# Fetching the first MLP's inputs apart from the addition of their halves, and starting those additions later in attention

## The chip, the cores and the metric

The kernel runs on one core of a Trainium2 chip. A core has engines that run side by side, each with its own queue of instructions in order: TensorE (PE: matmuls; its weight loads are listed as PEld), VectorE (DVE), ScalarE (ACT), GpSimd (POOL), and SyncE (SP), whose queue here only issues DMA transfers between DRAM and the core's memory. Engines wait for each other through semaphores. The metric is the device time of one execution in microseconds.

## The reference

Attention with a memory term over 4 batches, 8 heads, 576 positions and head width 64, then two MLPs over the 2304 tokens (512 wide, 2048 hidden), the first with an ELU and the second with a leaky ReLU. All inputs are float32.

```python
scores = scale * q @ k^T                      # causal mask
a = softmax(scores); local = a @ v
q_p = phi(q)                                  # elu(q) + 1
mem_out = (q_p @ M_prev) / (q_p . z_prev + 1e-06)
x = g * mem_out + (1 - g) * local             # 2304 x 512
h = x @ moe_w_in;  x = where(h > 0, h, exp(min(h, 0)) - 1) @ moe_w_out
h = x @ moe2_w_in; out = max(0.01 * h, h) @ moe2_w_out
```

## The kernel before

**Numbers.** Products are made from float32 operands cut into a high part (`xh`, `gh`, ...) and the rest (`xl`, `gl`, ...), with three matmuls for one product (high by high, by the weights' rest, rest by high). Batch 0's attention runs in plain float32 (`V32 = 1`), the other batches' attention with the cut.

**Attention.** Each batch is one token tile `ti` of 576 tokens; its 8 heads are taken as 4 pairs `hp`. Per head and group of queries there are scores (L426, L427), the exponentials on DVE (L429), transposes of the probabilities (L455), and the product with the values in `pv` (L522), whose accumulator `po` goes through a copy `xp` to DRAM. In batch 0 that is ACT's copy and a write into `xm` (L527). In the other batches the accumulator holds two products whose sum is the output; DVE copies it (L529) and SP writes it into `xq` (L530), one buffer per head of the pair, so the reader has to add two halves. `k_unit`, `q_unit` and `qp_unit` prepare keys and queries (L292 to L341; DVE makes the rests there, `kl` L300, `qs` L341, `qpl` L248).

**The first MLP's first part.** It takes 7 of the 16 hidden blocks (`NFA`) and is filled into attention, because PE is not kept busy by attention alone. `phase1_units(ti)` makes a list of units for one batch's two parts of 288 tokens. Before the change, each part has:

- `u_x`: fetch, addition and cut. Batch 0: one DMA `x<-xm` (L675, 576 KB). Others: four DMAs, two halves into `x` (L681) and two into `y` (L682), 288 KB each, then four additions `x<-x,y` on DVE (L684), one per 128 rows of the 512. Then `split_x`: four casts `xh` on ACT (L239 inside `copy`), four subtractions `xl` on POOL (L609), and the writes of both to DRAM for the MLP's second part (L670).
- seven `u_h`: 12 matmuls each into a bank `pm` (L616), then the ELU (ACT twice at L629, DVE at L630) and the cut of the result into `gh` and `gl`.
- four `u_o`: 21 matmuls each (L644), a copy and a write of `ys` (L697).

The tiles `x` and `y` have one buffer each (`mtile("x", 1, ...)`), so a part's fetch into them waits until the part before has been read out of them.

**What sets the order.** The attention units come as one list with a cost each; `pos` is the sum of the costs so far (in ns of PE). When a batch's last attention unit is passed (`done`), its MLP units are appended to `fill`, due at `pos + DELAY` (13000). From that point each attention unit adds `c * rate` to a credit, and a unit of `fill` is emitted as soon as it is due and its cost is covered; units with cost 0, as `u_x`, go at once when they are first in the list. Units of `fill` are emitted with a raised priority (`FILL_OFF = 20`). That is the order in which the code is written. The Tile scheduler then orders each engine's queue itself, by priority and by its own times of when operands are ready, so the order in the program can differ from the order of emission.

The lines that place the units:

```python
        if done is not None:
            fill += [(pos + DELAY, c2, u2) for c2, u2 in phase1_units(done)]
        if fill and fill[0][0] <= pos:
            credit += c * rate
        while fill and fill[0][0] <= pos and fill[0][1] <= credit:
            _, c2, u2 = fill.pop(0)
            credit -= c2
            with tc.high_priority(offset=FILL_OFF):
                u2()
```

What is left of `fill` when attention ends is run with the loading of more weights; then come the rest of the first MLP and the second MLP, to the end.

## Time and profile before

| | us |
|---|---|
| median of three runs | 1096.52 |
| lowest, highest | 1096.45, 1099.43 |
| the profiled execution | 1098.26 |
| its span (first to last instruction) | 1096.2 |
| PE busy in it | 1057.6 (96%) |
| DVE, ACT, POOL busy | 600.3, 484.8, 530.6 |
| mean granted clock of TensorE, share of full | 0.995 |

The profiled execution is one more run, with 2.06 us outside its span. The busy share is an average over stages. The first 385 us or so hold attention with the first MLP filled in between; after it there is little but MLP. So the table of windows (busy time by stretch), the timelines of PE, DVE and SP with what ended each wait, and the DMA issues with their time to landing are what to read for this change.

### The profile page before, as it was taken

What the parts mean: (1) busy time and instruction counts of PE and PEld (TensorE: products, weight loads), DVE (VectorE), ACT (ScalarE), POOL (GpSimd) and SP (SyncE); (2) the same over time, 40 slices, a digit from 0 to 9 for tenths busy, and PEclk for the clock granted to TensorE, in tenths of its full rate; (3) what the DMA queues carried; (4) which work ended last, traced back from release to release, by engine and by line L of the source; (5) the groups of instructions that cost most, each with busy time, mean ns of one, the idle gap of its engine ahead of it and who ended that gap; (6) DMA issues with size and microseconds to landing.
All of it is one profiled execution on the core that took longest, in us unless ns stands there. A gap on an engine that the chain in (4) does not pass through costs nothing.

```text
span 1096.2 us, 17406 instructions
## 1 busy us (share of the span) xinstructions
PE 1057.6 (96%) x5904; PEld 912.7 (83%) x5904; DVE 600.3 (55%) x1398; ACT 484.8 (44%) x1169; POOL 530.6 (48%) x674
## 2 busy tenths in 40 slices
PE   6998899989998999999999999999999999999997
PEld 3777789979998999978877889888888888888896
DVE  6889987778878857566574314664321222232232
ACT  5988877777877645444343223432211110111110
POOL 7675675667667626455453224755422322222221
PEclk9999999999999999999999999999999999999999
DMA  7753643564365139665653304331200100010010
GB/s 181 189 144 91 188 115 99 124 169 145 78 178 156 59 81 271 225 215 185 219 189 119 98 18 116 135 116 39 77 1 1 58 20 1 1 39 1 1 39 20
DMA packets 151576, 115.05 MB, mean 105 GB/s; under 512 B 81728, under 2 KB 144192, under 8 KB 151488
## 3 DMA queue, kind: packets, MB, share of 16 engines
q1 hardware_dynamic: 151488, 113.95, 35.5%
q8 instruction: 47, 0.77, 0.3%
q14 instruction: 41, 0.34, 0.1%
HBM read 78.52 MB, written 31.85 MB: 101 GB/s over the span
## 4 chain that ended last, share of the span: by engine, by line
PE 73%; DMA 8%; DVE 7%; POOL 3%; ACT 3%; SPq 3%; issue 3%; DVEq 0%; POOLq 0%; ACTq 0%
PE pm L616 17%; PE sc L876 14%; PE tp L616 13%; PE sc L644 8%; PE po L876 4%; PE pm L644 4%; PE po L522 3%; PE tp L455 3%; PE po L644 2%; DMA wraw<-in_moe_w_out_dram 2%; DMA x<-xq 2%; SPq L212 2%; PE sc L426 1%; PE sc L427 1%; PE pm L522 1%
## 5 line engine op out<-in xcount | busy, mean ns | idle before, releaser
L623 POOL TENSOR_TENSOR gl<-e,gh 128x512 fp32r<-128x512 f32 (+2 forms) x181 | 199.8, 1108 | 369.8 <-DVE gh L241 291.9
L616 PE MATMUL tp<-xw,w 128*128 128x512 f32 (+1 forms) x504 | 145.4, 371 | 0.9 <-DVE e L630 0.9
L616 PE MATMUL pm<-xw,w 128*128 128x512 f32 (+1 forms) x496 | 143.9, 371 | 0.0
L876 PE MATMUL sc<-w,gh 128*128 128x512 f32 x448 | 137.7, 393 | 0.0
L449 POOL TENSOR_SCALAR pt<-pt,rs,omg 128x128 f32<-128x128 f32 (+4 forms) x160 | 102.7, 651 | 28.0 <-DVE rs L444 25.7
L616 PEld LDWEIGHTS tp<-xw,w 128*128 128x128 f32 x504 | 91.3, 188 | 19.7 <-DVE e L630 1.7
L644 PE MATMUL sc<-gh,w 128*128 128x512 f32 (+2 forms) x438 | 106.0, 343 | 1.1 <-DVE st L857 0.7
L616 PEld LDWEIGHTS pm<-xw,w 128*128 128x128 f32 x496 | 90.5, 188 | 18.5
L434 ACT ACTIVATE pt<-pt,mx 128x128 f32<-128x128 f32 (+4 forms) x160 | 93.2, 585 | 22.7 <-DVE mx L429 22.1
L876 PEld LDWEIGHTS sc<-w,gh 128*128 128x128 f32 x448 | 83.1, 188 | 17.9
L616 PE MATMUL tp<-xv,w 128*128 128x512 f32 (+1 forms) x252 | 93.2, 370 | 0.0
L616 PE MATMUL pm<-xv,w 128*128 128x512 f32 (+1 forms) x248 | 92.0, 371 | 0.0
L616 PE MATMUL pm<-xh,w 128*128 128x288 f32 x368 | 80.2, 305 | 9.1 <-DVE e L630 5.7
L635 ACT ACTIVATE e<-pm 128x512 f32<-128x512 f32 (+1 forms) x40 | 22.2, 556 | 150.3 <-PE pm L616 149.1
L455 PE MATMUL tp<-ident,pt 128*128 128x128 f32 x480 | 80.1, 276 | 8.0 <-DVE al L248 3.1
L241 DVE CAST gh<-e 128x512 fp32r<-128x512 f32 (+2 forms) x146 | 77.9, 537 | 16.9 <-PE po L644 4.2
L137 POOL TENSOR_TENSOR w<-wm,w 128x512 fp32r<-128x512 f32 x50 | 66.1, 1344 | 43.4 <-ACT w L239 43.4
L876 PE MATMUL sc<-w,gl 128*128 128x512 f32 x224 | 85.4, 393 | 0.0
L644 PEld LDWEIGHTS sc<-gh,w 128*128 128x128 f32 x438 | 74.6, 188 | 12.2 <-issue 1.5
L636 DVE TENSOR_TENSOR e<-tp,e 128x512 f32<-128x512 f32 (+1 forms) x40 | 25.5, 637 | 107.2 <-ACT e L635 107.1
L636 DVE TENSOR_TENSOR e<-pm,e 128x512 f32<-128x512 f32 (+1 forms) x40 | 25.5, 637 | 105.8 <-ACT e L635 105.8
L429 DVE CUSTOM_DVE_ANT_0 pt<-sc,mask 128x128 f32<-128x128 f32 (+4 forms) x160 | 69.4, 446 | 8.6 <-PE sc L427 4.3
(155 smaller groups left out, 2407.9 us busy)
## 6 DMA issues: line engine op xcount, KB each, us to landing
wraw<-in_moe_w_in_dram SPq DMA_DIRECT2D x32, 512.0 KB, 4.1
wraw<-in_moe_w_out_dram SPq DMA_DIRECT2D x32, 512.0 KB, 5.3
xh<-xh SPq DMA_DIRECT2D x8, 576.0 KB, 3.3
xl<-xl SPq DMA_DIRECT2D x8, 576.0 KB, 3.9
ys<-st SPq DMA_DIRECT2D x32, 144.0 KB, 3.0
x1s<-st SPq DMA_DIRECT2D x36, 128.0 KB, 1.9
x<-x1s SPq DMA_DIRECT2D x9, 512.0 KB, 3.9
out_dram<-st SPq DMA_DIRECT2D x36, 128.0 KB, 1.7
```

The costliest lines, as they stand in the source:

```text
L137: nc.gpsimd.tensor_tensor(out=w[:, 1, a], in0=t[:, a], in1=_f(w)[:, 0, a], op=ALU.subtract)
L241: (nc.vector if eng == "V" else nc.gpsimd).tensor_copy(dst, src)
L429: nc.vector.tensor_tensor_reduce(out=pt[0:m, k0:k0 + n], in0=sc[0:m, 0:n], in1=mk, op0=ALU.add, op1=ALU.min, scale=-0.125, scalar=mx[0:m, ...
L434: nc.scalar.activation(out=pt[0:m, 0:nk], in_=pt[0:m, 0:nk], func=AF.Exp, scale=-1.0, bias=mx[0:m, last:last + 1], accum_out=self.pd["ss"] ...
L449: nc.gpsimd.tensor_scalar(out=pt, in0=pt, scalar1=rs[0:m, i:i + 1], scalar2=omg[0:m, h:h + 1], op0=ALU.mult, op1=ALU.mult,)
L455: nc.tensor.transpose(dst, self.p[c][:, k0:k0 + kn], ident)
L522: nc.tensor.matmul(po[:, a:b], w, x, start=i == 0, stop=i == len(mms) - 1)
L616: nc.tensor.matmul(ph, wi[:, wj, kc, :], xx[:, kc, :], start=n_mm == 0, stop=n_mm == 11)
L623: nc.gpsimd.tensor_tensor(out=gl, in0=g, in1=_f(gh), op=ALU.subtract)
L636: nc.vector.tensor_tensor(out=t, in0=ph, in1=t, op=ALU.max)
L644: nc.tensor.matmul(py, wo[:, wj, ec * P:(ec + 1) * P], gg, start=opens and f == first and n_mm == 0, stop=closes and f == last and n_mm == 2,)
L876: nc.tensor.matmul(pos[tb], gg[:, tb * P:(tb + 1) * P], wo[:, wj, :], start=f == 0 and n_mm == 0, stop=f == NF - 1 and n_mm == 2,)
```

## The change

Fetching and adding become two functions. `u_load` allocates the tiles and issues the DMAs. `u_x` does the additions (for batches with halves), the cut and its writes. The list of units begins with `u_x` of the first part; the second part's `u_load` stands after the first part's second `u_h` (f = 1), and its `u_x` after the first part's sixth (f = 5). Before, the second part's `u_x` with all its DMAs stood behind the four `u_o` of the first. `phase1_units` now returns the first part's `u_load` beside the list, and the main loop calls it at the moment the batch's attention is done, at ordinary priority. From batch 1 on the list is due at `pos + LATE` (20000) instead of `pos + DELAY` (13000); batch 0 keeps 13000. The number of instructions of each kind is the same.

```diff
+    LATE = 20000.0
...
-            def u_x(pi=pi, o=o, w=w, st=st):
-                def split():
-                    st["x"] = split_x(xt, w, pi % 2)
...
-                xt = mtile("x", 1, F32, (NKC, NW))[:, :, 0:w]
-                if ti < V32:
-                    nc.sync.dma_start(xt, xm_scr[ti][:, :, o:o + w])
-                    split()
-                    return
...
-                for c in range(NKC):
-                    nc.vector.tensor_tensor(out=xt[:, c], in0=xt[:, c], in1=x2[:, c], op=ALU.add)
-                split()
+        mine = [(pi, o, w, {}) for pi, (pt, o, w, _) in enumerate(parts) if pt == ti]
+
+        def u_load(pi, o, w, st):
+            xt = st["t"] = mtile("x", 1, F32, (NKC, NW))[:, :, 0:w]
+            if ti < V32:
+                nc.sync.dma_start(xt, xm_scr[ti][:, :, o:o + w])
+                return
+            x2 = st["t2"] = mtile("y", 1, F32, (NKC, NW))[:, :, 0:w]
+            for j in range(2):
+                ps, pz = slice(64 * j, 64 * j + 64), slice(64 - 64 * j, 128 - 64 * j)
+                nc.sync.dma_start(xt[ps], xq_scr[ti][j][ps, :, o:o + w])
+                nc.sync.dma_start(x2[ps], xq_scr[ti][j][pz, :, o:o + w])
+
+        def u_x(pi, o, w, st):
+            xt = st["t"]
+            if ti >= V32:
+                for c in range(NKC):
+                    nc.vector.tensor_tensor(out=xt[:, c], in0=xt[:, c], in1=st["t2"][:, c], op=ALU.add)
+            st["x"] = split_x(xt, w, pi % 2)
+            for n in range(2):
+                nc.sync.dma_start(xp_scr[n][pi], _f(st["x"][n]))
+            st["g"] = {}
+
+        units = [(0, lambda: u_x(*mine[0]))]
+        for k, (pi, o, w, st) in enumerate(mine):
...
             for f in range(NFA):
                 units.append((HC * 12 * w / 2.4, lambda f=f, u=u_h: u(f)))
+                if k + 1 < len(mine) and f == 1:
+                    units.append((0, lambda k=k: u_load(*mine[k + 1])))
+                if k + 1 < len(mine) and f == NFA - 2:
+                    units.append((0, lambda k=k: u_x(*mine[k + 1])))
...
-        return units
+        return lambda: u_load(*mine[0]), units
...
-            fill += [(pos + DELAY, c2, u2) for c2, u2 in phase1_units(done)]
+            fetch, more = phase1_units(done)
+            fetch()
+            start = pos + (DELAY if done < V32 else LATE)
+            fill += [(start, c2, u2) for c2, u2 in more]
```

What this makes of the program's order is shown at three places. A row is a line of the kernel, an operation, what it writes and reads, and its shape. Lines of the changed kernel are one higher up to L660 (L528 is L527 of before, L617 is L616, L645 is L644, L249 is L248, L430 is L429), the fetches are L666, L671 and L672, the additions L678, the writes of the cut L681.

**Batch 0's first fetch, SP's queue.** `xm` is what batch 0's attention writes, `x` the tile of the MLP's input; `kn`, `vn`, `qn` and `kk` belong to the attention of batch 1, and `xq` is its output. Before:

```order
L212 DMA vn<-in_v_dram 128x2x64 x3
L530 DMA xq_0_86<-xp 128x320
L217 DMA vn<-in_v_dram 64x2x64 x2
L227 DMA zb<-in_z_prev_dram 128x256
L530 DMA xq_1_87<-xp 128x256
L675 DMA x<-xm_80 128x4x288
L212 DMA kn<-in_k_dram 128x3x64 x2
L530 DMA xq_1_87<-xp 128x320
```

After:

```order
L213 DMA kn<-in_k_dram 128x3x64
L528 DMA xm_80<-xp 64x320
L300 DMA kk_1537<-kk_1537 64x256
L300 DMA kk_1537<-kk_1537 64x320
L666 DMA x<-xm_80 128x4x288
L213 DMA kn<-in_k_dram 128x3x64
L300 DMA kk_1538<-kk_1538 64x256
L531 DMA xq_0_86<-xp 128x256
```

The fetch `x<-xm` stood 17 rows behind the last write of `xm`, between `xq` writes of batch 1's second head; now it stands three rows behind it.

**The end of batch 0's MLP and the beginning of batch 1's, PE and DVE.** On PE, L644 (after: L645) are the last output matmuls of batch 0, and L616 with `xh0_3624` (after: L617 with `xh0_3774`) the first of batch 1's; the others are attention's. PE before:

```order
L644 MATMUL pm_3589<-gh_3061,w4_792 128x288 x2
L644 MATMUL pm_3589<-gl_3062,w4_792 128x288
L644 MATMUL pm_3589<-gh_3130,w5_904 128x288 x2
L644 MATMUL pm_3589<-gl_3131,w5_904 128x288
L644 MATMUL pm_3589<-gh_3192,w6_1009 128x288 x2
L644 MATMUL pm_3589<-gl_3193,w6_1009 128x288
L616 MATMUL pm_3666<-xh0_3624,w0_200 128x288 x2
L522 MATMUL po_3423<-qph_3037,ms0_164 128x320
L522 MATMUL po_3423<-qpl_3038,ms0_164 128x320
```

PE after, where batch 0's matmuls end:

```order
L645 MATMUL pm_3595<-gl_3137,w5_904 128x288
L329 MATMUL po_3045<-ident_66,ph_e_2823 128x128 x2
L645 MATMUL pm_3595<-gh_3198,w6_1009 128x288 x2
L645 MATMUL pm_3595<-gl_3199,w6_1009 128x288
L427 MATMUL sc_3388<-kk0_3160,qs0_3228 128x448
L428 MATMUL sc_3388<-kl0_1_175,qs0_3228 128x448
L456 MATMUL tp_3299<-ident_66,pt21_182 128x128
L456 MATMUL tp_3299<-ident_66,pt3_3153 128x128
L456 MATMUL tp_3299<-ident_66,pt4_3202 128x128
```

PE after, 26 rows further down, where batch 1's begin:

```order
L456 MATMUL tp_3373<-ident_66,pt3_3153 128x128
L456 MATMUL tp_3373<-ident_66,pt4_3202 128x128
L523 MATMUL po_3109<-qph_3043,ms0_164 128x256
L523 MATMUL po_3109<-qpl_3044,ms0_164 128x256
L523 MATMUL po_3109<-dh2_152,vv_2844 128x256 x2
L523 MATMUL po_3109<-dl2_154,vv_2844 128x256 x2
L293 MATMUL sc_3574<-ident_66,kn_3269 128x128 x3
L617 MATMUL pm_3812<-xh0_3774,w0_200 128x288 x2
L617 MATMUL pm_3874<-xh0_3774,w1_390 128x288 x2
```

L616 stood directly behind the last L644; now 33 rows with 40 matmuls of attention lie between. On DVE, the additions of batch 1's first part (L684, after: L678) in the same place, with their neighbours. DVE before:

```order
L529 COPY xp_3219<-po_3207 128x320
L248 TENSOR_TENSOR al_3298<-tp_3333,ah_3297 128x320
L429 ISA pt4_3387,mx_3388<-sc_3389,mask_128 128x288
L429 ISA mx_3388 128x1
L248 TENSOR_TENSOR dl2_154<-tp_3361,dh2_152 128x384
L429 ISA pt0_3450,mx_3451<-sc_3452,mask_128 128x128
L429 ISA mx_3451 128x1
L429 ISA pt4_3387,mx_3388<-sc_3393,mask_128,mx_3388 128x288
L429 ISA mx_3388 128x1
L684 TENSOR_TENSOR x_3614<-x_3614,y_3615 128x288 x4
L529 COPY xp_3353<-po_3346 128x256
```

DVE after:

```order
L430 ISA pt0_3456,mx_3457<-sc_3458,mask_128 128x128
L430 ISA mx_3457 128x1
L430 ISA pt1_3478,mx_3479<-sc_3480,mask_128 128x256
L430 ISA mx_3479 128x1
L249 TENSOR_TENSOR al_3304<-tp_3339,ah_3303 128x320
L678 TENSOR_TENSOR x_3030<-x_3030,y_3031 128x288 x4
L249 TENSOR_TENSOR qpl_3044<-po_3092,qph_3043 128x320
L430 ISA pt21_182,mx_3550<-sc_3551,mask_128 64x320
L430 ISA mx_3550 64x1
```

Both copies `xp` in the piece of before belong to batch 2. The last one of batch 1, whose write the fetch has to wait for, stands 47 rows ahead of the additions before and 24 rows ahead of them after, outside of both pieces. Behind the additions stood a copy `xp`; now `qpl` stands there, which PE's L523 of the piece above reads.

**Batch 1's second part, DVE.** L684 (after: L678) are its additions, L630 (after: L631) the ELU of the first part's hidden blocks. DVE before:

```order
L429 ISA pt3_3821,mx_3822<-sc_3823,mask_128 128x448
L429 ISA mx_3822 128x1
L684 TENSOR_TENSOR x_4507<-x_4507,y_4508 128x288 x2
L630 SCALAR_TENSOR_TENSOR e_3852<-e_3852,pm_3839 128x288
L429 ISA pt4_3828,mx_3829<-sc_3830,mask_128 128x288
L429 ISA mx_3829 128x1
L684 TENSOR_TENSOR x_4507<-x_4507,y_4508 128x288 x2
L248 TENSOR_TENSOR al_3743<-tp_3738,ah_3742 128x320
```

DVE after:

```order
L249 TENSOR_TENSOR al_3706<-tp_3701,ah_3705 128x320
L430 ISA pt4_3786,mx_3787<-sc_3792,mask_128,mx_3787 128x288
L430 ISA mx_3787 128x1
L445 RECIPROCAL rs_3739<-rs_3739 128x2
L678 TENSOR_TENSOR x_3895<-x_3895,y_3896 128x288 x4
L631 SCALAR_TENSOR_TENSOR e_3954<-e_3954,pm_3941 128x288
L430 ISA pt0_3845,mx_3846<-sc_3847,mask_128 128x128
L430 ISA mx_3846 128x1
```

The additions stood two and two around an ELU; now they are in one piece, between attention's L445 and an ELU. Counted on PE's queue, 9 matmuls stood between the last DMA into `x` and the first of these additions, and now 47.

## Rows read from the trace of the kernel before

**Rows 1.** Page, busy time of the engines, share of the span, instructions.

```profile
PE 1057.6 (96%) x5904; PEld 912.7 (83%) x5904; DVE 600.3 (55%) x1398; ACT 484.8 (44%) x1169; POOL 530.6 (48%) x674
```

**Rows 2.** Windows: busy (count) of PE, PEld, DVE, ACT, POOL; clock, DMA share, GB/s.

```profile
102.00:120.00 18.00, 14.99 (x98) 12.27 (x98) 17.56 (x59) 13.08 (x38) 11.75 (x23) 1.00 0.56 140
160.00:200.00 40.00, 39.88 (x310) 39.48 (x310) 30.44 (x97) 29.71 (x86) 25.28 (x42) 1.00 0.38 100
216.00:234.00 18.00, 15.18 (x112) 13.90 (x111) 11.49 (x37) 11.30 (x34) 9.47 (x17) 1.00 0.72 191
234.00:250.00 16.00, 13.40 (x88) 12.51 (x87) 13.16 (x39) 13.26 (x38) 11.65 (x17) 0.89 0.62 158
318.00:330.00 12.00, 10.88 (x84) 10.45 (x83) 9.06 (x27) 7.14 (x22) 9.17 (x13) 1.00 0.78 216
330.00:342.00 12.00, 9.17 (x60) 8.92 (x60) 8.97 (x22) 7.90 (x23) 7.51 (x12) 0.86 0.85 242
```

**Rows 3.** SP timeline, last writes and fetches of batches 0 and 1: start, duration, transfer.

```profile
101.74 0.48 SPq L527 DMA_DIRECT2D xm<-xp  x1
...
116.09 0.55 SPq L675 DMA_DIRECT2D x<-xm  x1
...
199.72 0.32 SPq L530 DMA_DIRECT2D xq<-xp  x1
...
214.12 0.54 SPq L681 DMA_DIRECT2D x<-xq  x1
```

**Rows 4.** DMA issues: transfer, queue, count, size, median us to landing.

```profile
xq<-xp SPq DMA_DIRECT2D x24, 160.0 KB, 2.1
...
x<-xm SPq DMA_DIRECT2D x2, 576.0 KB, 4.8
...
xm<-xp SPq DMA_DIRECT2D x8, 80.0 KB, 2.1
```

**Rows 5.** DVE timeline, additions of batches 1 and 2; brackets: idle time before, releaser.

```profile
221.29 2.17 DVE L684 TENSOR_TENSOR x<-x,y 128x288 f32<-128x288 f32 x4 [4.79 <-issue]
...
243.25 0.83 DVE L684 TENSOR_TENSOR x<-x,y 128x288 f32<-128x288 f32 x2 [2.07 <-DMA x<-xq]
...
320.03 0.83 DVE L684 TENSOR_TENSOR x<-x,y 128x288 f32<-128x288 f32 x2 [2.38 <-DMA y<-xq]
...
335.18 2.16 DVE L684 TENSOR_TENSOR x<-x,y 128x288 f32<-128x288 f32 x4 [2.87 <-DMA y<-xq]
```

**Rows 6.** PE timeline, waits at the MLP's inputs in batches 0 to 2.

```profile
121.37 0.81 PE L616 MATMUL pm<-xh,w 128*128 128x288 f32 x4 [1.85 <-ACT xh L239]
...
222.27 0.53 PE L616 MATMUL pm<-xh,w 128*128 128x288 f32 x2 [1.52 <-ACT xh L239]
...
223.85 0.42 PE L522 MATMUL po<-qph,ms 128*128 128x320 f32 x1 [1.05 <-DVE xp L529]
...
244.50 0.53 PE L616 MATMUL pm<-xh,w 128*128 128x288 f32 x2 [2.59 <-DVE e L630]
...
323.68 0.52 PE L455 MATMUL tp<-ident,pt 128*128 128x128 f32 x3 [1.12 <-DVE al L248]
...
338.16 0.85 PE L616 MATMUL pm<-xh,w 128*128 128x288 f32 x2 [2.83 <-DVE e L630]
```

**Rows 7.** Line L239 by form, casts of xh on ACT: min/median/max ns.

```profile
L239 ACT CAST xh<-x x32: 421/432/442, 120.9 to 432.4; 128x288 fp32r<-128x288 f32 x32
```

**Rows 8.** Lines L681 and L682 (halves into x and y): landing times.

```profile
DMA to landing us min/median/max: 3.8/4.2/8.8
...
DMA to landing us min/median/max: 4.0/4.6/9.6
```

**Rows 9.** DVE groups: busy us, mean ns of one, idle before, releasers.

```profile
L429 DVE CUSTOM_DVE_ANT_0 pt<-sc,mask 128x128 f32<-128x128 f32 (+4 forms) x160 | 69.4, 446 | 8.6 <-PE sc L427 4.3 <-PE tp L455 1.9 <-ACT ac L245 0.7
...
L248 DVE TENSOR_TENSOR al<-tp,ah 128x320 fp32r<-128x320 f32 x48 | 22.4, 482 | 3.2 <-ACT ah L247 3.0
...
L429 DVE DVE_READ_ACCUMULATOR2_ANT mx<- 128x1 f32 (+1 forms) x192 | 15.4, 80 | 0.0
```

14 lines of the change are left out of this document (removed).

## The prediction

> **What bounds the kernel now.** I first read the busy table of the page: TensorE (PE) works 1057.6 us of a span of 1096.2, 96%, which leaves 38.6 us of idle time [rows 1]. The change adds or removes no instruction; it moves them. What it can win is therefore PE's idle time and what a lower clock costs. The window table shows where PE idles inside attention: 102 to 120 us (14.99 busy of 18), 216 to 234 (15.18 of 18), 234 to 250 (13.40 of 16), 318 to 330 (10.88 of 12) and 330 to 342 (9.17 of 12) [rows 2]. In contrast, from 160 to 200, with attention and the first MLP mixed, PE is busy 39.88 of 40 [rows 2]. With a wait of 1.85 at 121 [rows 6] these stretches lose 3.01 + 1.85 + 2.82 + 2.60 + 1.12 + 2.83 = 14.2 us. The same table gives the granted clock: 1.00 everywhere but in 234 to 250 (0.89) and 330 to 342 (0.86) [rows 2]. Both hold a piece at the lower level, 1.2 of 2.4 GHz: 0.11 x 16 and 0.14 x 12 are 1.7 us of clock lost each time. In both PE had waited for VectorE (DVE), 2.59 and 2.83 us, longer than anywhere else in these stretches [rows 6]. With 2 x 1.7 the losses in reach are 17.6 us.
>
> Next, what ended these waits. PE waited for L616's operand (ACT's xh, 1.85 and 1.52 us), for DVE's xp copy (1.05) and twice for DVE's elu result e at L630 (2.59, 2.83) [rows 6]. The DVE timeline shows why DVE was late: it executes in order and stood idle before the additions L684, 4.79, 2.07, 2.38 and 2.87 us, mostly for the DMA of a half [rows 5]. So the additions matter where DVE has work behind them that PE wants soon: in both parts of batch 1 and of batch 2.
>
> **Batch 0: the fetch moves up.** It has one DMA and no additions. Before, SP issues it at 116.09 us, though the last xm write was issued at 101.74 [rows 3]; write and fetch take 2.1 and 4.8 us to land [rows 4]. Moved up to right behind the two kk copies that follow that write, the fetch waits on SP for the write to land, 101.74 + 2.1 = 103.8, and lands near 104.0 + 4.8 = 108.8. Behind it on SP stand kn loads, kk copies and an xq write; they wait about as long as the kk rows took anyway, so I charge nothing (about 0.5 us if not). An ACT cast of 0.43 later PE can begin, near 109.2 [rows 7]. In the new order L616's first matmul stands 67 attention matmuls further forward. At the rate of 102 to 120, 98 per 18 us = 5.44 per us [rows 2], that is 12.3 us before 119.5, where PE began to wait (121.37 less 1.85 [rows 6]): 107.2. So PE may stand about 2 us, less if its own order has lost time before; I take 1.5.
> What is won: these 67 matmuls no longer run alone. Lower price: PE's idle share of that window, 3.01/18 of 12.3 us = 2.1 us. Upper price: 67 x (1/5.44 - 1/7.75) = 3.7 us, with 310 per 40 us = 7.75 per us of the mixed window [rows 2]; part of that is smaller matmuls, so I take 2.8, the middle. Sum: -2.8 - 1.85 + 1.5 = **-3.2 us**, between -5.5 (3.7 and 1.85, no new wait) and 0 (2.1 and a new wait of 4).
>
> **Batch 1, first part: MLP work runs out.** The batch 0 units that started earlier also end earlier. In the new order PE has 40 attention matmuls with nothing between the last L645 of batch 0 and the first L617 of batch 1, and over the next 115 only 24 MLP matmuls where 49 stood. Before, L644 was followed directly by L616. Together some 83 attention matmuls lose their filler. At the two prices, 83/67 of 2.1 and of 3.7: 2.6 and 4.6 us; I take +3.5. For the upper end speaks that DVE is busy 17.56 of 18 us where attention runs alone [rows 2]. On the other side, before the last half was fetched at 214.12, though its write was issued at 199.72 [rows 3], and DVE came to the additions before it had landed. In the new order that fetch stands behind one load and the write itself: write 2.1 [rows 4], the two issues half a us each [rows 3], then 4.6 to land [rows 8], 7.7 us. L678 stands 24 DVE rows behind the last xp copy: of those between, eight read a sum in 0.08, one is a reciprocal, and fifteen others take about 0.45 to 0.5 by the commonest kinds [rows 9], 7 to 8 us. That covers the chain nearly, and the 4.79 us stall goes with what PE had of it, 1.52 + 1.05 [rows 6]. I take 0.4 as left over, so -2.2. Sum **+1.3 us**, from -1 (cheap mixing, no stall) to +6 (dear mixing and DVE standing as long as now).
>
> **Batch 1, second part.** Here the changed order does what it says: between the last x fetch and the first addition PE has 47 matmuls, where it had 9. At 7.75 per us that is 6.1 against 1.2 us, and the x halves, now ahead of six loads of vn on SP, need 3.8 to 8.8 us [rows 8]. A median landing of 4.2 is wholly hidden. So the 2.59 us and the clock behind them, 1.7, go, together -4.3; the four additions now stand in one block of 2.17 us [rows 5] in place of two and two, and L631's e waits behind it, for which I charge +0.8. Sum **-3.5 us**, -4.5 to -1.
>
> **Batch 2 and batch 3.** First part of batch 2: 18 matmuls between fetch and additions in both orders, so its 1.12 us [rows 6] stay: 0 (-1 to +1). Second part: 34 matmuls against 38, so the 2.87 us DVE stall stays or grows by half a us. But PE's first instruction that needs DVE behind the block is now L523 behind an xp copy, not L617, and that stands later. Half of the stall and one clock fall in two saved: -1.4 - 0.85, less the half us: **-1.7 us**, +1 to -4.5 (2.83 + 1.7). Batch 3: 19 matmuls in both and 68 against 64; PE is not waiting there now: 0.
> Sum: -3.2 + 1.3 - 3.5 - 1.7 = -7.1 us. On the profiled execution's own 1098.26 (span 1096.2 and 2.06 around it) that is 1091.2; it ran 1.74 above the median 1096.52, and on the median the forecast is **1089.4 us**.
>
> **A rule against the change.** For batch 1 the trace shows 5.44 matmuls per us alone and 7.75 mixed [rows 2]. The Trainium skill, Perfetto Trace Analysis, section Optimization Strategy, says that regimes in which different engines are the most contended may gain by interleaving. By that rule the thin stretch would be charged at its upper price and stands as the first rival; that DVE is at 98% in one and 76% in the other of these windows agrees with it [rows 2].
>
> **Rivals.** First: the unmixed stretch only changes place. Batch 0 wins its lower price (-2.1 - 0.35 for the waits), batch 1 pays its upper (+4.6 - 2.2), batch 1's second part gives -3.5, batch 2 nothing: -3.5, **1093.0 us**. For it: the amount of attention and MLP is the same in both orders. Against: the waits of batch 1 and 2 are no matter of mixing.
> Second, on the other side: batch 1's first fetch lands late. A half has taken 9.6 us [rows 8], 5.0 more than the median. DVE then stands in front of L678, with L249's qpl behind it, for which PE's next L523 waits, and no MLP matmul is at hand to fill PE. To the first rival's -3.5 come +5.0, a clock fall of 1.7 (both stalls that long had one) and 1.8 that the second part no longer wins: +5.0, **1101.5 us**. With the clock fall the change is a loss from a stall of some 2 us there, and a measurable one from some 3.3 us (-3.5 + 3.3 + 1.7 + 1.8 = +3.3). For it: the 216 to 234 window has the DMA engines 72% busy against 38% in 160 to 200 [rows 2]. Against: that cover of 7 to 8 us of DVE work.
> Third: the change doesn't place the additions further back where the scheduler decides again. The counts above show so for batches 2 and 3; if batch 2 keeps all it loses, -5.4, **1091.1 us**.
> Fourth: transfers are short when issued apart. Then batch 0's new wait, the left-over 0.4 and batch 2's stalls with their clock all go: -1.5 - 0.4 - 1.1 - 2.8 below the forecast, **1083.6 us**. The rows speak against it: halves of 64 x 4 x 288 numbers need 3.8 us at the least and 4.2 to 4.6 in the middle [rows 8], and nothing thins the traffic around them. The Trainium skill, DMA: Bandwidth & Descriptors, section Anatomy of one DMA, fits 2.0 us plus bytes over 436e3 per us; for 294912 bytes that would be an estimated 2.7 us, and by it the sum would be this rival's. The trace's 3.8 to 9.6 disagrees, and it decides.
>
> **How the numbers follow.** Chances: forecast 0.44, the first rival 0.20, the late landing 0.14, the unmoved additions 0.14, short transfers 0.08. About 0.3%, 3.3 us, is what a measurement of this kernel can tell from no change: 1093.2 to 1099.8 is "same". Faster: 0.40 + 0.07 + 0.11 + 0.08 = 0.66; same: 0.04 + 0.12 + 0.03 + 0.01 = 0.20; slower: 0.01 + 0.13 = 0.14. The range leaves out most of the late landing (0.13) and half of the short transfers (0.04): 1084 to 1099.
>
> **What would show it.** Right: the first L617 near 109 us; PE's wait at batch 1's second part and the clock fall behind it gone; PE busy under 88% for some 20 us around batch 1's first L617, the price of batch 0's lead. Wrong: a wait on DVE of over 3 us before L678 in batch 1 with the clock at its lower level behind it; or both clock falls still there, which would mean that the fetches' lead, not the place of the additions, was all that moved. The forecast falls if PE's idle time before 130 us does not shrink by 2 us at least.

## The result, and the profile after

The changed kernel takes 1105.38 us in the median (1103.11 to 1106.92) against 1096.49, a ratio of 1.0077 with a 95% interval of 1.0048 to 1.0106. Measured again in ten executions beside 31 of the kernel before it was 1104.01 against 1097.98, 1.0048 (1.0033 to 1.0063). So it is slower by some 5 to 9 us, where 7.1 us less had been forecast; the range ended at 1099.

The profiled execution took 1106.92 us, 1105.0 in its span. The busy table of the page:

```profile
PE 1062.9 (96%) x5904; PEld 920.9 (83%) x5904; DVE 599.9 (54%) x1398; ACT 482.7 (44%) x1169; POOL 531.5 (48%) x674
```

PE is busy for 5.3 us more than in [rows 1], with the same number of matmuls, and idle for 3.5 us more. The windows tell where, and why busy time grew (busy and count of PE, PEld, DVE, ACT, POOL, then granted clock, DMA share, GB/s):

```profile
102.00:120.00 18.00, 14.94 (x101) 14.37 (x102) 15.92 (x48) 12.60 (x36) 12.55 (x20) 0.91 0.65 186
120.00:140.00 20.00, 18.01 (x127) 17.19 (x126) 15.83 (x44) 17.47 (x53) 15.03 (x24) 0.91 0.55 162
160.00:200.00 40.00, 40.00 (x313) 39.82 (x312) 34.19 (x107) 32.81 (x97) 26.32 (x41) 1.00 0.35 89
216.00:234.00 18.00, 14.08 (x94) 13.37 (x94) 15.83 (x39) 10.85 (x31) 12.02 (x19) 0.91 0.75 189
234.00:250.00 16.00, 14.78 (x101) 14.38 (x102) 13.08 (x45) 13.52 (x42) 13.34 (x19) 0.89 0.40 118
250.00:270.00 20.00, 18.26 (x127) 17.61 (x126) 14.61 (x42) 12.09 (x34) 13.52 (x21) 0.91 0.41 119
318.00:330.00 12.00, 10.55 (x82) 10.27 (x82) 7.29 (x21) 7.75 (x23) 5.87 (x9) 1.00 0.69 144
330.00:342.00 12.00, 8.83 (x59) 8.52 (x59) 9.35 (x27) 7.46 (x21) 9.21 (x13) 0.85 0.91 261
342.00:360.00 18.00, 18.00 (x130) 17.89 (x129) 14.06 (x45) 15.20 (x46) 12.25 (x21) 0.91 0.34 110
```

Against [rows 2]: 102 to 120 shows the gain of batch 0's lead in 101 matmuls in place of 98, but at a clock of 0.91. In 216 to 234 PE is busy 14.08 us in place of 15.18. And the clock, below 1.00 in two of the windows before (1.7 us lost in each), is below it in seven here: (1 - clock) times the window's length is 1.6, 1.8, 1.6, 1.8, 1.8, 1.8 and 1.6, together 12.0 us against 3.4 (the last two windows share one longer fall, so they hold six falls). A matmul at half clock counts as busy for longer, hence the longer busy time. PE's timeline has the waits of these stretches (start, duration, line, operation; in brackets the idle time before and what ended it). A fall of the clock follows six of the eight, all but 1.18 and 1.45:

```profile
109.37 1.01 PE L617 MATMUL pm<-xh,w 128*128 128x288 f32 x4 [2.28 <-ACT xh L240]
...
128.82 1.01 PE L338 MATMUL sc<-ident,qn 128*128 128x128 f32 x5 [1.62 <-DVE mx L430]
...
218.36 0.39 PE L523 MATMUL po<-qph,ms 128*128 128x256 f32 x1 [3.88 <-DVE qpl L249]
...
233.06 0.41 PE L427 MATMUL sc<-kk,qs 128*128 128x320 f32 x1 [1.18 <-DVE qs L342]
...
235.14 0.47 PE L427 MATMUL sc<-kk,qs 128*128 128x448 f32 x1 [1.53 <-DVE mx L430]
...
255.90 0.55 PE L338 MATMUL sc<-ident,qn 128*128 128x128 f32 x3 [1.61 <-DMA qn<-in_q_dram]
...
325.55 0.41 PE L427 MATMUL sc<-kk,qs 128*128 128x320 f32 x1 [1.45 <-DVE mx L430]
...
339.34 0.58 PE L523 MATMUL po<-qph,ms 128*128 128x256 f32 x1 [3.17 <-DVE xp L530]
```

In batch 1 the waits of 1.52, 1.05 and 2.59 us [rows 6] are gone; the new ones are 3.88, 1.18, 1.53 and 1.61. DVE's timeline before the third and the last of these waits, where additions stand:

```profile
206.81 0.49 DVE L530 COPY xp<-po 128x320 f32<-128x320 f32 x1
...
213.35 0.48 DVE L249 TENSOR_TENSOR al<-tp,ah 128x320 fp32r<-128x320 f32 x1
...
215.74 2.16 DVE L678 TENSOR_TENSOR x<-x,y 128x288 f32<-128x288 f32 x4 [1.90 <-issue]
...
217.82 0.48 DVE L249 TENSOR_TENSOR qpl<-po,qph 128x320 fp32r<-128x320 f32 x1
...
336.60 2.16 DVE L678 TENSOR_TENSOR x<-x,y 128x288 f32<-128x288 f32 x4 [1.95 <-DMA qn<-in_q_dram]
...
338.79 0.49 DVE L530 COPY xp<-po 128x320 f32<-128x320 f32 x1
```

The last xp copy of batch 1 ends at 207.3. DVE has work up to 213.83, idles 1.90, adds for 2.16, and only then makes qpl, for which PE has stood since 214.48. The operand of qpl that ACT makes, qph, was ready at 213.15, so it was its place behind the additions that kept qpl back:

```profile
212.73 0.42 ACT L248 CAST qph<-po 128x320 fp32r<-128x320 f32 x1
```

The SP timeline has the chain of that idle time: the write of the copy, the fetches of x and y behind it.

```profile
208.24 0.56 SPq L531 DMA_DIRECT2D xq<-xp  x1
...
210.35 0.54 SPq L671 DMA_DIRECT2D x<-xq  x1
...
210.94 0.60 SPq L672 DMA_DIRECT2D y<-xq  x1
```

The y half landed at 215.66, 4.72 us after its issue. It was not late; 4.6 is the median in [rows 8].

One more view is worked out from the trace of both kernels: the time at which PE begins the same amount of its work (for each matmul, the sum of what those before it in the queue take by their shape at the upper clock without waiting). It shows differences to the kernel before, in us, and the same for experiments that follow:

```
work  before   after  b0_fetch  b1_apart  b1_wact  act_writes
 50     95.3    -0.6     -0.5      +0.2     -0.6      -0.5
150    210.6    -3.4     -6.2      -5.0     -5.8      -5.2
170    234.8    +2.7     -3.2      +1.7     -0.8      -5.0
180    249.8    -1.4     -6.8      -2.4     -5.8      -5.8
190    260.0    +2.4     -6.9      +1.5     -5.2      -5.8
250    320.3    +3.2     -5.8      +1.5     -4.8      -5.3
270    346.6    +5.2     -7.8      -0.2     -7.9      -1.4
600    688.0    +8.9     -6.8      +4.0     -3.0      -1.3
```

The changed kernel leads by 3.4 us when batch 0's MLP ends, loses 6.1 at batch 1's first part, wins 4.1 where the kernel before stood in batch 1's second part, and loses 3.8 at once after it. From the 190th to the 270th us of work, up to and in batch 2, it loses 2.8 more, and another 3.7 behind attention, between the 270th and the 600th. There PE waits longer for DVE than before: 1.65 us for e near 428 (before 1.07, near 421), and 1.54 and 1.48 for st, where DVE adds the last part to an output (L863), near 548 and 684 (before no more than 0.43). That is one execution of each; the second profile of the changed kernel has the same losses within 0.3 us at the 170th, 190th, 270th and 600th us.

### The profile page after: what moved, and what is told of

Its sections match the earlier page's. It is cut to its first block, busy times and chain, and to the rows that moved or that the text cites. A ratio compares the mean times of both kernels' runs of the same rounds, so it can differ in the third digit from the quotient of the medians.

```text
span 1105.0 us, 17427 instructions
## 1 busy us (share of the span) xinstructions
PE 1062.9 (96%) x5904; PEld 920.9 (83%) x5904; DVE 599.9 (54%) x1398; ACT 482.7 (44%) x1169; POOL 531.5 (48%) x674
## 4 chain that ended last, share of the span: by engine, by line
PE 71%; DVE 7%; DMA 7%; issue 4%; ACT 4%; POOL 4%; SPq 2%; DVEq 0%; POOLq 0%; ACTq 0%
PE pm L617 17%; PE sc L882 14%; PE tp L617 13%; PE sc L645 7%; PE po L882 4%; PE po L523 3%; PE tp L456 3%; PE pm L645 3%; PE po L645 2%; POOL w L138 2%; DMA x<-xq 1%; PE sc L427 1%; PE sc L428 1%; ACT pt L435 1%; PE pm L523 1%
## 5 line engine op out<-in xcount | busy, mean ns | idle before, releaser
L617 PE MATMUL tp<-xw,w 128*128 128x512 f32 (+1 forms) x504 | 145.7, 371 | 0.7 <-DVE e L631 0.7
L617 PE MATMUL pm<-xw,w 128*128 128x512 f32 (+1 forms) x496 | 143.9, 372 | 0.0
L450 POOL TENSOR_SCALAR pt<-pt,rs,omg 128x128 f32<-128x128 f32 (+4 forms) x160 | 105.3, 667 | 24.7 <-DVE rs L445 19.8
L645 PE MATMUL sc<-gh,w 128*128 128x512 f32 (+2 forms) x466 | 112.1, 341 | 3.6 <-DVE st L863 3.0
L617 PEld LDWEIGHTS tp<-xw,w 128*128 128x128 f32 x504 | 91.2, 188 | 19.5 <-DVE e L631 1.4
L617 PEld LDWEIGHTS pm<-xw,w 128*128 128x128 f32 x496 | 90.5, 188 | 18.4
L617 PE MATMUL tp<-xv,w 128*128 128x512 f32 (+1 forms) x252 | 93.2, 370 | 0.0
L617 PE MATMUL pm<-xv,w 128*128 128x512 f32 (+1 forms) x248 | 92.0, 371 | 0.0
L645 PEld LDWEIGHTS sc<-gh,w 128*128 128x128 f32 x466 | 79.1, 188 | 15.0 <-issue 3.8
L617 PE MATMUL pm<-xh,w 128*128 128x288 f32 x368 | 83.9, 314 | 2.6 <-ACT xh L240 2.3
L242 DVE CAST gh<-e 128x512 fp32r<-128x512 f32 (+2 forms) x146 | 74.1, 510 | 17.4 <-PE po L645 4.1
L430 DVE CUSTOM_DVE_ANT_0 pt<-sc,mask 128x128 f32<-128x128 f32 (+4 forms) x160 | 69.3, 445 | 11.1 <-PE sc L428 5.5
```

Of the source, the lines that this page charges most:

```text
L242: (nc.vector if eng == "V" else nc.gpsimd).tensor_copy(dst, src)
L430: nc.vector.tensor_tensor_reduce(out=pt[0:m, k0:k0 + n], in0=sc[0:m, 0:n], in1=mk, op0=ALU.add, op1=ALU.min, scale=-0.125, scalar=mx[0:m, ...
L450: nc.gpsimd.tensor_scalar(out=pt, in0=pt, scalar1=rs[0:m, i:i + 1], scalar2=omg[0:m, h:h + 1], op0=ALU.mult, op1=ALU.mult,)
L617: nc.tensor.matmul(ph, wi[:, wj, kc, :], xx[:, kc, :], start=n_mm == 0, stop=n_mm == 11)
L645: nc.tensor.matmul(py, wo[:, wj, ec * P:(ec + 1) * P], gg, start=opens and f == first and n_mm == 0, stop=closes and f == last and n_mm == 2,)
```

## The experiments

All ratios are to the kernel before, from 10 to 12 executions beside 31 to 35 of it, with 95% intervals. Rows were measured in four groups, each beside its own executions of the kernel before, so the difference of two rows can come out 1 to 2 us apart by medians and by ratios:

| kernel | median us | ratio | interval |
|---|---|---|---|
| b0_fetch | 1094.43 | 0.9976 | 0.9953 to 0.9999 |
| late_only | 1094.25 | 0.9972 | 0.9952 to 0.9991 |
| no_b0 | 1100.62 | 1.0017 | 0.9997 to 1.0036 |
| late13 | 1102.81 | 1.0049 | 1.0028 to 1.0069 |
| b23_apart | 1095.34 | 0.9974 | 0.9959 to 0.9990 |
| b1_apart | 1102.52 | 1.0050 | 1.0030 to 1.0070 |
| b0_late | 1099.87 | 1.0015 | 0.9996 to 1.0035 |
| pool_adds | 1101.06 | 1.0022 | 1.0005 to 1.0039 |
| b1_wact | 1097.60 | 0.9994 | 0.9965 to 1.0024 |
| b1_pool | 1100.51 | 1.0016 | 0.9995 to 1.0037 |
| b0_pool | 1104.04 | 1.0051 | 1.0031 to 1.0072 |
| b0_pool1 | 1096.15 | 0.9978 | 0.9956 to 1.0001 |
| act_writes | 1097.98 | 1.0004 | 0.9989 to 1.0018 |
| b1_fill | 1101.02 | 1.0035 | 1.0017 to 1.0053 |
| b0_wact | 1096.96 | 0.9986 | 0.9966 to 1.0007 |
| after_again | 1104.01 | 1.0048 | 1.0033 to 1.0063 |

### Which part of the change

**b0_fetch**, batch 0's early fetch alone; u_both is u_load and u_x in one unit (the diffs are cut, `...` marks where):

```diff
-        units = [(0, lambda: u_x(*mine[0]))]
...
+        solo = ti >= V32
+        units = [(0, lambda: (u_both if solo else u_x)(*mine[0]))]
...
+            if k:
+                units.append((0, lambda k=k: u_both(*mine[k])))
...
-            fetch()
-            start = pos + (DELAY if done < V32 else LATE)
+            if done < V32:
+                fetch()
+            start = pos + DELAY
```

> The kernel before with one part of the change: batch 0's first fetch issued when its attention ends. Theory (the lead starves the handover): the changed kernel was 3.4 us ahead at PE's 150th us of work and 2.75 behind at the 170th, because batch 0's MLP ran out before batch 1's inputs were there; then this kernel, in whose order 55 attention matmuls stand alone at that place (40 in the changed one, 0 before), gains 3 to 3.5 us up to the handover and gives back 6 or more there, with at least one more fall of the clock: 1098 to 1101. Rival (the lead is sound, the later and split additions are what costs): it keeps its gain, 1092 to 1094.

**no_b0**, the reverse: u_both for batch 0, the rest as changed.

```diff
-        units = [(0, lambda: u_x(*mine[0]))]
...
+        solo = ti < V32
+        units = [(0, lambda: (u_both if solo else u_x)(*mine[0]))]
...
-            fetch()
+            if done >= V32:
+                fetch()
```

> The changed kernel with batch 0 treated as before; batches 1 to 3 as changed. Theory (the lead starves the handover): MLP matmuls last up to batch 1's first part again (0 attention matmuls alone), PE's waits of 3.9 and 2.7 us there go with their two clock falls, and so does the 3.4 us lead; batch 1's first part should be no later than in the kernel before. What is left is the wait for qn behind the writes of the cut on SP (3.8 with its clock fall) and batch 2: 1096 to 1100, near before. Rival (the later and split additions cost): it loses what the changed kernel loses and lacks the lead, 1106 to 1109.

**late13**:

```diff
-    LATE = 20000.0
+    LATE = 13000.0
```

> The changed kernel with LATE at 13000, as the due time was before. Theory (the lead starves the handover): the order at batch 1's first part is the same as in the changed kernel (40 attention matmuls alone), so its 6 us are lost again; only batch 2's second part moves: 1102 to 1106. Rival (the later due time costs): 1095 to 1099.

**late_only**, in the kernel before:

```diff
-            fill += [(pos + DELAY, c2, u2) for c2, u2 in phase1_units(done)]
+            start = pos + (DELAY if done < V32 else LATE)
+            fill += [(start, c2, u2) for c2, u2 in phase1_units(done)]
```

> The kernel before with the later due time alone (20000 from batch 1 on). Theory (the lead starves the handover): nothing of batch 0 and batch 1's first part moves; 1095 to 1099, the difference being in batch 1's second part and batch 2. Rival (the later due time costs): 1101 to 1106.

The theory that batch 0's lead starves the handover fell: b0_fetch has 55 attention matmuls alone there, more than the changed kernel, and is 0.24% faster than the kernel before. Nor does the due time cost: late13 lies where after_again, the changed kernel measured again, does (1.0049, 1.0048), and late_only is faster. (late13 came out where the fallen theory had put it, but only because its order is the changed kernel's up to 226 us.) What late13 has and b0_fetch has not is the fetch apart from the additions in batches 1 to 3, 8.4 us by their medians. And no_b0, with no stretch alone at all, is no faster than the kernel before (interval 0.9997 to 1.0036). DVE and PE there:

```profile
208.03 2.16 DVE L678 TENSOR_TENSOR x<-x,y 128x288 f32<-128x288 f32 x4 [3.37 <-issue]
```

```profile
210.78 0.39 PE L427 MATMUL sc<-kk,qs 128*128 128x256 f32 x1 [2.67 <-DVE qs L342]
```

DVE stood before the additions again, and PE for what was queued behind them. In all these kernels DVE comes to the first part's additions in batch 1 soon after the last half's fetch was issued: 2.9 us after it in the changed kernel (210.94 to 213.84), 1.8 before (214.71 to 216.50), 1.4 in no_b0 (203.25 to 204.66). The half needs longer to land, 4.72 us in the changed kernel. So the code issues the fetch apart, but in the compiled order the additions still follow it closely. That the scheduler counts on a shorter landing is a likely reason, which no run shows. The split of a part's fetch and additions alone, without the first part's early fetch, was not run.

The next runs place the loss. **b1_apart** is b0_fetch with the fetch apart in batch 1, **b23_apart** in batches 2 and 3 (the same with `ti > 1` and `done > 1`). Against b0_fetch:

```diff
+        apart = ti == 1
...
-            if done < V32:
+            if done < V32 or done == 1:
                 fetch()
```

> Batch 0's early fetch, and in batch 1 alone the fetch apart from the additions (both parts), all due times at 13000. It is b0_fetch plus the change's treatment of batch 1. Theory (fetch apart costs in batch 1: DVE stands before the additions with qpl behind them, and the writes of the cut come ahead of qn's loads on SP): 5 to 7 us over b0_fetch, 1099 to 1102, with PE's waits of about 4 us at L523 and 1.7 us for qn again. Rival (the loss of the changed kernel is spread over batches 1 to 3, or comes from batch 2 and 3): within 3 us of b0_fetch, 1093 to 1097.

> b0_fetch plus the fetch apart from the additions in batches 2 and 3 alone, all due times at 13000. Theory (fetch apart costs in batch 1): within 2 us of b0_fetch, 1093 to 1097. Rival (it costs in batches 2 and 3): 1098 to 1102.

b1_apart has the whole loss (1.0050; the changed kernel 1.0048), b23_apart none (0.9974; b0_fetch 0.9976). That settles the place: what the change does in batch 1. The two kernels have the same order on DVE up to the qpl at 210.99 and on PE up to 212.6, so the stretch behind can be compared row by row. DVE in b0_fetch:

```profile
210.99 0.48 DVE L249 TENSOR_TENSOR qpl<-po,qph 128x320 fp32r<-128x320 f32 x1
...
215.50 0.46 DVE L678 TENSOR_TENSOR x<-x,y 128x288 f32<-128x288 f32 x1 [2.52 <-DMA y<-xq]
```

and in b1_apart:

```profile
214.73 2.16 DVE L678 TENSOR_TENSOR x<-x,y 128x288 f32<-128x288 f32 x4 [2.41 <-issue]
...
216.82 0.48 DVE L249 TENSOR_TENSOR qpl<-po,qph 128x320 fp32r<-128x320 f32 x1
```

DVE stands before the additions in both, 2.52 and 2.41 us. But the qpl of 128 x 320 is made ahead of them in b0_fetch, at 210.99, and behind them in b1_apart, at 216.82. PE's waits in b0_fetch:

```profile
217.56 0.47 PE L427 MATMUL sc<-kk,qs 128*128 128x288 f32 x1 [2.70 <-DVE mx L430]
...
229.14 0.41 PE L427 MATMUL sc<-kk,qs 128*128 128x320 f32 x1 [0.91 <-DVE qs L342]
```

and in b1_apart:

```profile
217.35 0.39 PE L523 MATMUL po<-qph,ms 128*128 128x256 f32 x1 [4.41 <-DVE qpl L249]
...
232.07 0.42 PE L427 MATMUL sc<-kk,qs 128*128 128x320 f32 x1 [1.18 <-DVE qs L342]
...
234.16 0.47 PE L427 MATMUL sc<-kk,qs 128*128 128x448 f32 x1 [1.52 <-DVE mx L430]
...
254.97 0.55 PE L338 MATMUL sc<-ident,qn 128*128 128x128 f32 x3 [1.62 <-DMA qn<-in_q_dram]
```

That is 2.70 + 0.91 against 4.41 + 1.18 + 1.52, and then 1.62 for qn, a wait that b0_fetch doesn't have. Between 216 and 270 us the clock falls once in b0_fetch and three times in b1_apart.

**b0_late** joins the two parts that were faster alone (against b0_fetch):

```diff
-            start = pos + DELAY
+            start = pos + (DELAY if done < V32 else LATE)
```

> The kernel before with the two parts that each were faster alone: batch 0's early fetch and the due time of 20000 from batch 1 on; additions with their fetches, as before. If the two gains add: 1089 to 1092. Rival (the later due time works only through batch 0's old start, or the gain of each is within one execution's spread): 1093 to 1096.

They do not add: 1.0015. In that order PE waits 4.31 us for batch 1's first xh, which is made from those additions:

```profile
219.11 1.33 PE L617 MATMUL pm<-xh,w 128*128 128x288 f32 x4 [4.31 <-ACT xh L240]
```

### What in batch 1

**pool_adds** and **b1_pool** take the additions away from DVE, in the changed kernel and in b1_apart's batch 1 (there with `nc.gpsimd if ti == 1 else nc.vector`):

```diff
-                    nc.vector.tensor_tensor(out=xt[:, c], in0=xt[:, c], in1=st["t2"][:, c], op=ALU.add)
+                    nc.gpsimd.tensor_tensor(out=xt[:, c], in0=xt[:, c], in1=st["t2"][:, c], op=ALU.add)
```

> The changed kernel with the four additions of a part on POOL in place of DVE. Theory (PE waits since DVE stands before the additions, with attention's work behind them): DVE is free, PE's wait of 3.9 us at batch 1's first part and of 3.2 at batch 2's second fall under 1.5 each, with their clock falls: 1095 to 1101. Rival (PE is short of matmuls that are ready, whoever adds): the waits stay at 3 us or more and POOL's later gl adds to them: 1104 to 1110.

> b1_apart with batch 1's additions on POOL. Theory (PE waits at the first part since DVE stands before the additions with qpl and the exponentials behind them): the 4.4 us wait at L523 and the 2.7 us that follow fall to 2 or less together, one clock fall in place of two; 4 to 7 us under b1_apart, 1096 to 1099. Rival (the thin stretch without MLP matmuls is what PE loses, and it is longer here, 53 matmuls in place of 40): 1101 to 1105.

PE's waits in pool_adds at the two places:

```profile
218.91 0.53 PE L617 MATMUL pm<-xl,w 128*128 128x288 f32 x2 [1.99 <-POOL xl L610]
...
336.22 0.53 PE L617 MATMUL pm<-xh,w 128*128 128x288 f32 x2 [2.03 <-DVE e L631]
```

Up to the additions DVE's order in pool_adds is the changed kernel's, and PE's is the same up to 219.8 us. The wait of 3.88 for qpl is gone, with 1.99 for xl left, and in place of 3.17 there is 2.03. Both stay above the 1.5 that were expected. 53 attention matmuls stand alone in this order. pool_adds is 1.0022; that interval overlaps after_again's at its end, the medians are 3 us apart. b1_pool lies 2.0 us under b1_apart by the medians and 3.7 by the ratios, where 4 to 7 were expected: its waits at the first part are 1.97, 0.55, 0.47 and 0.58, but it has a new one of 1.48 for qpl at 245, and in batch 2 one of 3.31 for xh where b1_apart has 1.41. So the local reading holds, and the total is mixed with what the new order does elsewhere.

**b1_wact** and **act_writes** move the writes of the cut to another queue, in b1_apart's batch 1 (`nc.scalar if ti == 1 else nc.sync`) and in all of the changed kernel:

```diff
-                nc.sync.dma_start(xp_scr[n][pi], _f(st["x"][n]))
+                nc.scalar.dma_start(xp_scr[n][pi], _f(st["x"][n]))
```

> b1_apart with the writes of batch 1's cut issued from ACT's queue in place of SP's. Theory (two separate costs in batch 1: DVE standing before the additions, and qn's loads held up on SP behind the write of xh): the waits at the first part (4.4 and 2.7 us, two clock falls) stay, the wait of 1.6 us for qn near 255 and the clock fall behind it go: 3 to 3.5 us under b1_apart, 1098 to 1100. Rival (qn is late for another reason, the DMA engines or the place of its issue): the wait stays and the time is b1_apart's, 1101 to 1104.

> The changed kernel with the writes of the cut of all parts issued from ACT's queue in place of SP's. Theory (qn's loads are held up behind the write of xh on SP): 3 to 5 us under the changed kernel, as b1_wact was 5 us under b1_apart. Rival (that gain belonged to b1_wact's own order, and elsewhere the writes take time from ACT): within 2 us of the changed kernel.

Both expectations take it that the write of xh holds up qn's loads on SP. Whether it does can be read from the traces. qn has one buffer (`bufs=1` in `load_qk`), so the loads for the next pair of heads must wait until `ph_f` on DVE (L386; L385 before) has read the pair before. `ph_f` needs `ph_e` from ACT, and that tile must first have been read by PE's L329 (L328 before). The changed kernel, on PE, DVE and SP:

```profile
245.66 0.49 PE L329 MATMUL po<-ident,ph_e 128*128 128x128 f32 x3
...
251.25 0.81 DVE L386 SCALAR_TENSOR_TENSOR ph_f<-qn,ph_e 128x640 f32<-128x640 f32 x1
...
243.80 0.34 SPq L681 DMA_DIRECT2D xh<-xh  x1
...
252.72 1.65 SPq L213 DMA_DIRECT2D qn<-in_q_dram  x3
```

and the kernel before:

```profile
231.96 0.55 PE L328 MATMUL po<-ident,ph_e 128*128 128x128 f32 x3
...
239.82 0.82 DVE L385 SCALAR_TENSOR_TENSOR ph_f<-qn,ph_e 128x640 f32<-128x640 f32 x1
...
240.71 2.00 SPq L212 DMA_DIRECT2D qn<-in_q_dram  x4
```

Before, `ph_f` ended at 240.64 and qn's loads went out at 240.71, ahead of the write of xh at 246.84. Changed, the write stands ahead of them, and SP, which had issued vn's last load by 238.98, sends nothing until 243.80. But the write was gone 8 us before `ph_f` ended at 252.06; the loads follow 0.66 us later, behind a kk copy, and PE stands for them from 254.29. So it was not the write's place on SP that made qn late. (no_b0, with the writes on SP and the fetch apart, has no wait for qn.) It was `ph_f`, since L329 ends at 246.15 in place of 232.51. PE had no wait between 235.14 and 254.29; L329 only stands later in its order. PE's waits in b1_wact:

```profile
216.20 0.58 PE L523 MATMUL po<-qph,ms 128*128 128x256 f32 x1 [4.10 <-DVE qpl L249]
...
225.76 0.41 PE L338 MATMUL sc<-ident,qn 128*128 128x128 f32 x2 [0.73 <-DMA qn<-in_q_dram]
...
231.96 0.41 PE L427 MATMUL sc<-kk,qs 128*128 128x320 f32 x1 [1.08 <-DVE qs L342]
```

and its `ph_f` and qn's loads:

```profile
244.44 0.92 DVE L386 SCALAR_TENSOR_TENSOR ph_f<-qn,ph_e 128x640 f32<-128x640 f32 x1
...
245.42 2.00 SPq L213 DMA_DIRECT2D qn<-in_q_dram  x4
```

The first, 4.10, stayed, as expected, and the wait near 255 is gone, since `ph_f` ends at 245.36 and the loads go out at 245.42. (The 0.73 at 225 is for the loads of the pair before.) SP stood there as long without the write: from 237.64 to 244.42 in b1_wact and from 236.10 to 243.21 in act_writes. Not expected: of the 2.7 us that followed the first wait only 1.08 remained. b1_wact is 4.9 us under b1_apart by the medians and 6.1 by the ratios, act_writes 6.0 and 4.8 under after_again (1.0004 against 1.0048, intervals apart). One wait of 1.6 and its clock fall, 1.8, explain 3.4 of that. What the edit changed besides the queue is the order: PE's in b1_wact is another than b1_apart's from 224.8 us on, in act_writes another than the changed kernel's from 115 us on. So moving the writes gained, but the gain belongs to the orders that came of it; that a write on SP held up loads is not shown.

**b1_fill** was to part a wait from the clock that falls behind it:

```diff
+            if pr.ti == 2 and pr.hp == 0 and j == 0 and gi == 0:
+                for _ in range(16):
+                    nc.tensor.matmul(po[:, 0:128], ident, ident, start=True, stop=True)
```

> b1_apart with 16 matmuls of the identity by itself put directly before the L523 matmuls that wait 4.4 us for qpl at batch 1's first part; they write an accumulator that the next matmul starts anew, so they change no result. They fill PE's wait without shortening it. Theory (a wait costs a second time by the clock that falls behind it): the clock stays at its upper level behind this wait, and of the 3.4 us at half rate 1.7 come back, 0.5 to 2 us under b1_apart, though more matmuls are executed. Rival (the clock's fall has nothing to do with PE standing): the fall near 218 stays, and the time is b1_apart's or 1 to 2 us above it.

```profile
216.92 5.20 PE L524 MATMUL po<-ident 128*128 128x128 f32 x32 [4.31 <-DVE qpl L249]
```

It did not fill the wait: the first of the added matmuls waited for qpl as well, 4.31 us, the clock fell, and the 5 us of matmuls came behind. The question stays open. What it shows instead: 4.95 us of PE's work at this place cost nothing that can be measured (1.0035 against 1.0050). Behind it one wait of 1.09 is left of 1.18 and 1.52, the 1.62 for qn is gone, and between 234 and 270 us the clock stays at 1.00, where b1_apart has two falls. But from 218 to 219 us on the orders of DVE, ACT and SP are others than b1_apart's too, so this is not the effect of the added work alone.

### Versions meant to be faster

**b0_pool** is b0_fetch with all additions on POOL, **b0_pool1** with those of batch 1, **b0_wact** with the writes on ACT's queue. This is the edit of b0_pool1; those of the other two are as in pool_adds and act_writes:

```diff
-                    nc.vector.tensor_tensor(out=xt[:, c], in0=xt[:, c], in1=st["t2"][:, c], op=ALU.add)
+                    (nc.gpsimd if ti == 1 else nc.vector).tensor_tensor(out=xt[:, c], in0=xt[:, c], in1=st["t2"][:, c], op=ALU.add)
```

> b0_fetch with the additions of all parts on POOL; fetches with their additions, as before. A version meant to beat both kernels. If PE's waits beside the additions come from DVE standing: below b0_fetch, 1089 to 1093. Rival (POOL is late with gl instead, 69 attention matmuls stand alone at batch 1): 1094 to 1099.

> b0_fetch with batch 1's additions alone on POOL. Batch 1's first part as in b0_pool, the other batches as in b0_fetch: 1090 to 1094 if DVE's standing in batch 1 is what is left to win, 1094 to 1098 if the thin stretch decides.

> b0_fetch with the writes of the cut on ACT's queue: the part of the change that gained, and the repair that helped batch 1. A version meant to beat both kernels. If SP's queue holds up loads there too: 1088 to 1093. Rival (with fetch and additions together the writes stand behind qn's loads already, nothing to win): 1093 to 1097.

None beats b0_fetch. b0_pool is slower (1.0051); its profile has waits of 1.24 us for xl and 0.66 for gl, both POOL's, and 3.10 for e, between 414 and 479; b0_pool1 and b0_wact are b0_fetch's equals within their intervals. By their ratios four kernels are 2.4 to 3.1 us under the kernel before: b0_fetch, late_only, b23_apart and b0_pool1, the last with an interval that just reaches 1.

The changed kernel itself, measured as the others were:

> The changed kernel itself, in as many rounds as the others, so that their differences to it can be taken from one kind of measurement. Expected at a ratio of 1.005 to 1.010 to the kernel before (1.0077 in the four runs at first). If it lay at 1.004 or less, the later due time would cost nothing beside late13 (1.0049).

## Why the prediction was wrong

Term by term, by the table on the same work: batch 0 -3.2 forecast and -3.4 found; batch 1's first part +1.3 and +6.1; its second part -3.5 and -0.3 (-4.1, then +3.8); the way to batch 2 and batch 2 -1.7 and +2.8; behind attention nothing and +3.7. The sum is -7.1 forecast and +8.9 in this profile.

**Batch 0** was right in its mechanism. Forecast: fetch landed at 108.8, a new wait of up to 2 us, -3.2 us in all. Found: landed at 108.86, PE waiting 2.28 for xh, -3.4 us by the time its MLP ends, and a kernel with this part alone is 0.24% faster, 2.6 us. That -3.2 met -3.4 so closely is partly luck: a clock fall behind the new wait, in one of two executions, was not in the sum, and b0_fetch leads by 6.2 us at the same place. The list of losses also counts some 0.5 us twice, as the wait of 1.85 begins at 119.52, within the window to 120. The last sign that the prediction named fails as it was written: PE's idle time before 130 us shrank by 1.0 us only (16.28 to 15.27), not by 2. Busy time did not measure the lead there.

**Batch 1, first part**, is the step that failed most: +1.3 forecast, +6.1 found. Two things in it were wrong. The chain of the fetch was put at 7.7 us and the DVE work that covers it at 7 to 8; the trace has 8.4 (207.3 to 215.66) and 6.5 (to 213.83), so 1.90 us of stall in place of 0.4. That is small. The larger error: "the 4.79 us stall goes" was priced by what PE had lost to the old one, 1.52 + 1.05. A stall costs by what stands behind it. Before, that was an xp copy, which PE wanted late; now it is qpl, and PE wanted it 1.26 us before the additions began. So the additions themselves and qpl counted too: 1.26 us, 2.08 from the first addition to qpl's start, 0.54 to PE's, together 3.88. The order rows ahead of the prediction showed qpl there, and the second rival named it; the sum did not use it. b0_fetch against b1_apart shows it, the same stall with qpl ahead and behind, and so does pool_adds, where the wait for qpl is gone with the additions taken off DVE. Two clock falls came with it in the changed kernel. The sign that was to show this term wrong, a wait of DVE of over 3 us, looked at the wrong engine: DVE waited 1.90 us and PE 3.88. The price for the stretch without MLP, +3.5, was not tested apart; b0_fetch, with the longer stretch, loses 3.0 us over these 20 us of work in its profile, waits and a clock fall included, so 3.5 was not too low.

**Batch 1, second part**: the forecast part came true (DVE's idle time before the additions 0.00, the wait for e and the clock fall behind it gone, -4.1 us). But +3.8 a few us later ate the gain: PE's wait for qn, 1.61, with a clock fall of 1.8 behind it. The prediction had no term for attention's own loads being placed elsewhere. qn's loads came 12 us later than before, since `ph_f`, which frees their one buffer, did. Why the scheduler put L329 and with it `ph_f` later is not shown. That moving the writes to ACT's queue took the wait away (b1_wact, act_writes) shows that the order depends on them, not that they blocked the queue.

**Batch 2**: -1.7 forecast; +2.0 found in the profile from 250 to 270 us of work, and 0.8 from 190 to 250, with a PE wait of 3.17 for an xp copy behind the additions. The argument "PE needs DVE behind the block later" was false: PE was there at 336.17, the block ended at 338.76. But b23_apart shows no cost of batches 2 and 3, and late13 beside after_again none of the due time, so this wait is one order's own: after_again, with the same order, has it again, 3.45, and late13 doesn't.

**Behind attention**, +3.7 in this profile and +3.8 in after_again's, stands in no term. Its waits for e and st are named above; what brought them about was not tested.

**The rivals.** The second had the right sign, place and nearly the size (1101.5), with the wrong cause: no transfer was late. The third was right about the means in batch 1's first part: the additions did not move back there. The first, zero-sum mixing, fell with b0_fetch. The fourth fell by the halves' landings in the changed kernel, 3.8 to 4.7 us in batch 1's first part as in [rows 8]; the 2.7 that had been estimated by the Trainium skill, DMA: Bandwidth & Descriptors, section Anatomy of one DMA, is again under what the trace shows. That section gives its fit for the transfers that GpSimd issues; these are issued from SP, so the fit did not speak of them. The slower side had 0.14 of the chances, since the waits that the change adds were taken as small remainders of their own; six of the eight waits in the changed kernel's timeline had a fall of the clock behind them, 1.6 to 1.8 us each and 3.4 for the last, and the sum charged the clock only where it had already fallen before.

What stays open: how the loss divides between the waits and the clock (in the windows above the clock alone lost 8.6 us more than before, of a span 8.8 us longer, and no run parts the two); what places L329 later; what the 3.7 us behind attention come from; and why the due time of 20000 gains alone and not with batch 0's lead beyond what b0_late's rows show.

## What to carry to other kernels

Price a wait on an in-order engine by the first instruction behind it that the bound engine wants, and add the whole block that stands between; how long the engine itself idles says little. When a load comes late, look up what frees its buffer before blaming what stands ahead of it in the queue: here an edit to the queue helped, and yet the late load had gone out within 0.7 us of the moment its one buffer was free. Where a scheduler places the instructions, issuing a transfer earlier in the code doesn't widen its distance to the consumer: look at the distance in the compiled order, and change the parts of a change one batch at a time. Compare where the orders of two kernels first differ: only up to there, and in the rows just behind, does an edit show what its text says.
